# A token assignment that counts on 128 columns and searches in five steps instead of six

## The chip, the cores and the metric

The kernel runs on one core of a Trainium2 chip. The metric is the device time of one execution in microseconds (us); less is better. TensorE (PE) does matrix products, VectorE (DVE), ScalarE (ACT) and GpSimd (POOL) do elementwise work, SyncE (SP) issues the transfers.

## The reference

Three stages follow one another. Only the third one's token assignment is touched by the change.

```python
def _moe2_ref(x, w_gate, w1, w2):
    N, D = x.shape              # 2304 tokens, 512
    E = w_gate.shape[1]         # 8 experts
    cap = N // E                # 288 tokens each
    logits = x @ w_gate
    flat = logits.flatten()
    order = np.argsort(-flat)
    assigned = -np.ones(N, dtype=np.int64)
    counts = np.zeros(E, dtype=np.int64)
    for idx in order:           # the greatest logit first
        tok, e = (int(idx) // E, int(idx) % E)
        if assigned[tok] >= 0 or counts[e] >= cap:
            continue
        assigned[tok] = e
        counts[e] += 1
        if (assigned >= 0).all():
            break
    for e in range(E):
        mask = assigned == e
        h = np.maximum(x[mask] @ w1[e], 0.0)
        out[mask] = h @ w2[e]
```

Ahead of it stand an attention with decay (`x`), and a dense layer `x = leaky(x @ w_in) @ w_out` with 2048 hidden columns.

## The kernel before, in words

The products are made in pairs of rounded parts (`wh`, `gh` high parts, `gl` the remainder), three products for one. The stage that matters here begins when the gate logits `W0` stand (128 partitions x 8 experts x 18 tokens) and ends when the rows of `x2d`, the dense layer's output, and the list `ids` of each expert's tokens are both there; then the first expert gathers its rows.

Two streams share TensorE in this stage. One is `deferred`: 864 products of 512 columns, `acc<-wh,gh` and `acc<-wh,gl`, which make the second half of the dense layer. Each twelve of them need one pair of `gh` (a cast on ACT, L446) and `gl` (a subtraction on POOL, L447). Every other bank of them leaves through `xo` (L1006) to `x2d`.

The other is `routing`. It takes seven phases and a last, shorter one. In each phase every token bids for its best open expert, and a threshold is searched for in the bids' 32-bit keys, in two halves of the key (L1263). A search step compares the 18 keys of each partition with K candidate values on DVE (`r_ge`, L1266), counts with 18 small products on PE (`q_ct`, stationary `r_ge`, moving `r_oh` of 8 columns), tests the counts on DVE (`r_jk`, `r_most`, `r_found`) and sums the found candidates on PE (`q_base`, one product with the stationary `r_unit`). The next compare reads `q_base`. Before, a half has three steps with K of 63, 31 and 31, so a phase has six. After the second half come two counting products (`q_misc`, with `r_on` and `r_tru`) and about twenty small DVE operations that set up the next phase; the last of them is `r_oh`. After the phases, `q_misc` with `r_tri` and 18 products with `r_ob` make the list `ids`.

PE runs in program order. The order is set by numbers: `routing` is a generator that yields, ahead of each of its PE groups, an estimate in ns of the DVE work that precedes the group, and the caller deals products of `deferred` for it (L1057 to L1060):

```python
for ns in routing(nc, rt, ids, ps, W0, mm, vec):
    slack += 1.62 * ns
    while slack > 108 and next(rest, None):
        slack -= 216
```

So in front of a 31-column count stand 8 products of 512 columns, in front of `q_base` 3 or 4, and between two phases 39. What is left over is dealt after `ids`.

Of the kernel before, what the change touches and what calls it, by code (L numbers as in the profile page):

```python
# [14 lines left out]
BF = mybir.dt.bfloat16  # L15
I32 = mybir.dt.int32
AF = mybir.ActivationFunctionType
OP = mybir.AluOpType
# [33 lines left out]
SB = 4  # L52
PBUF = 4
ZG = 60


class InOrder:
# [162 lines left out]
def tile_kernel(ctx, tc, q, k, v, f, w_in, w_out, w_gate, w1, w2, out):  # L220
# [788 lines left out]
    with ExitStack() as c2:  # L1009
        g1p = c2.enter_context(tc.tile_pool(name="g1", bufs=1, reuse_waits="tile"))  # L1010
        g1 = [g1p.tile([128, NF, GT], FT, name=f"g1_{g}") for g in range(NG)]
        psa = c2.enter_context(tc.tile_pool(name="psa", bufs=1, reuse_waits="tile", space=PSUM))
        W0 = cst.tile([128, E, NT], FT, name="W0")
        with tc.tile_pool(name="ps2", bufs=1, reuse_waits="tile", space=PSUM) as psp, \
                tc.tile_pool(name="raw2", bufs=1, reuse_waits="tile") as rawp:
            raw[:] = rawp, W64[2]
            ps = {t: (lambda t=t, n=n: psp.tile([128, 512], FT, name=t, tag=t, bufs=n)) for t, n in (("h", 2), ("T", 2))}
            plan = Plan()
            op = plan.op
            plan.depth = {"T": 2, "h": 2, "x": 2, "w64": W64[2], "wsq": 1, "wbits": 2, "wst": 2, "w": WB, "wt": 1, "wq": 1}  # L1020
            plan.chained = dict.fromkeys(("x", "w64", "wsq", "wbits", "wst", "w", "wt", "wq"))
            for c in range(NC):
                wi[c]["ops"], wi[c]["wb"] = [], []
            wo = [w_out_ops(op, 1, jj, Z2[0] + Z2[1] * jj, "vec", ps) for jj in range(NF // 2)]
            wo0 = [again_ops(op, wod[jj], ZG, "vec") for jj in range(NF // 4)]
            gate = [y for s in wo for y in s["gate"]]
            lasts = []
            for g in range(NG):
                z = 10 * g
                X, loads, xb = x_ops(op, lambda: xp, g, z - 15) if g else (x0[0], [], op("vec", 0, lambda: None, (), -1e6, ["x"]).got)  # L1030
                need = []
                for j in range(NF):
                    need.append(leaky_ops(op, ps, "h", wi, j, lambda X=X: X, (loads, xb), z, z + j, lambda g=g, j=j: g1[g][:, j, :], (), [])[0])
                z = max(z + 8, Z2[2] + Z2[3] * g)
                lasts.append(logits_ops(op, ps, [lambda g=g, i=i: g1[g][:, 2 * i:2 * i + 2] for i in range(NF // 2)], NF, gate + need, [], z, z, g, False))
            lp = psa.tile([128, 512], FT, name="acc", tag="acc", bufs=ACB)

            def tokens(g):
                for i in (2 * g, 2 * g + 1):
                    pe.matmul(lp[:, E * i:E * i + E], L[:, 128 * i:128 * i + 128], sel, start=True, stop=True)  # L1040
            o = [op("pe", 430, lambda g=g: tokens(g), lasts[g:g + 1], 200) for g in range(NG)]
            op("vec", 215, lambda: vec.tensor_copy(W0, lp[:, :NT * E].rearrange("p (i e) -> p e i", e=E)), o, 200)
            run(plan)
        xpool.__exit__(None, None, None)
        lpool.__exit__(None, None, None)
        ps = c2.enter_context(tc.tile_pool(name="ps2b", bufs=1, reuse_waits="tile", space=PSUM))
        gtp = c2.enter_context(tc.tile_pool(name="gt2", bufs=1, reuse_waits="tile"))
        rt = c2.enter_context(tc.tile_pool(name="rt", bufs=1, reuse_waits="tile"))

        def mm(*a, **k):  # L1050
            tc.keep_in_program_order(PE.matmul(*a, **k))  # L1051

        ids = cst.tile([96, NTOK // 96], I32, name="ids")
        wo0 += [{"w": split_weights([(0, 1024, wod[jj])], V)} for jj in range(NF // 4, NF // 2)]
        rest = deferred(ps, mm)
        slack = 0
        for ns in routing(nc, rt, ids, ps, W0, mm, vec):  # L1057
            slack += 1.62 * ns
            while slack > 108 and next(rest, None):
                slack -= 216  # L1060
        for _ in rest:
            pass

# [103 lines left out]
def routing(nc, wk, ids, ps, W0, mm, vec):  # L1167
# [9 lines left out]
    def T(n, *shape, dt=FT, bufs=1):  # L1177
        return wk.tile([128, *shape], dt, name="r_" + n, tag="r_" + n, bufs=bufs)

    def Q(n, w, bufs=1):  # L1180
        return ps.tile([128, w], FT, name="q_" + n, tag="q_" + n, bufs=bufs)
# [9 lines left out]

    io = T("io", 96)
    G.iota(io, pattern=[[1, 96]], base=0, channel_multiplier=0, allow_small_or_imprecise_dtypes=True)
    steps = []
    unit = T("unit", 128, dt=BF)
    found = T("found", 1, dt=BF)
    G.memset(found, 0.0)
    on = T("on", 128, dt=BF)
    G.memset(on, 1.0)
    for i, (stp, K) in enumerate(((1024.0, 63), (32.0, 31), (1.0, 31))):  # L1200
        t = T(f"step{i}", K)
        V.tensor_scalar(t, io[:, 1:K + 1], stp, None, op0=OP.mult)
        G.memset(unit[(0, 64, 96)[i]:], stp)
        steps.append((K, t, (0, 64, 96)[i]))
    we = T("we", E)
    V.tensor_scalar(we, io[:, :E], -1.0, float(E), op0=OP.mult, op1=OP.add)
    eo = T("eo", E)
# [2 lines left out]
    G.affine_select(tri, on, pattern=[[1, 128]], base=0, channel_multiplier=-1, compare_op=OP.is_gt, fill=0.0)  # L1210
    tru = T("tru", 128, dt=BF)
    V.tensor_tensor(tru, on, tri, op=OP.subtract)
    seg = T("seg", E, NT)
    G.memset(seg, 1.0)
    G.memset(seg[:, :, 0:1], 0.0)

    yield 2500
    As = T("A", E, NT, dt=BF)
    G.memset(As, 0.0)
    U = T("U", NT)  # L1220
# [14 lines left out]
    for ph in range(E):  # L1235
# [16 lines left out]
        V.tensor_scalar(k1, b, 31, -0x80000000, op0=OP.arith_shift_right, op1=OP.bitwise_or)  # L1252
        V.tensor_tensor(k1, b, k1, op=OP.bitwise_xor)
        k2 = T("k2", 2, NT, dt=I32)
        V.tensor_scalar(k2[:, 0], k1, 16, None, op0=OP.logical_shift_right)
        V.tensor_scalar(k2[:, 1], k1, 0xffff, None, op0=OP.bitwise_and)
        kf = T("kf", 2, NT)
        V.tensor_copy(kf, k2)
        key = kf[:, 0]
        for half in range(2):  # L1260
            base = None
            for n, (K, kt, at0) in enumerate(steps):
                ct = Q("ct", 512, 2)[:, :E]  # L1263
                ge = T("ge", NT, 63, dt=BF)
                s = [128, NT, K]
                V.scalar_tensor_tensor(ge[:, :, :K], key[:, :, None].to_broadcast(s), base if n else 0.0,  # L1266
                                       kt[:, None, :].to_broadcast(s), op0=OP.subtract, op1=OP.is_ge)
                yield 500 + 19 * K
                for i in range(NT):
                    mm(ct[:K], ge[:, i, :K], oh[:, :, i], start=i == 0, stop=i == NT - 1)  # L1270
                jk, most = T("jk", E), T("most", 1)
                V.tensor_tensor_reduce(out=jk[:K], in0=ct[:K], in1=nr[:K], scale=1.0, scalar=-3e38, op0=OP.add, op1=OP.max, accum_out=most[:K])
                V.tensor_scalar(found[at0:at0 + K], most[:K], 0.0, None, op0=OP.is_ge)
                base = Q("base", 512)[:, 0:1]
                yield 430
                mm(base, unit[:at0 + K], found[:at0 + K], start=True, stop=True)
            yield 480 * (half == 0)
            if half == 0:
                k3 = T("k3", NT)
                V.tensor_scalar(k3, key, base, 131072.0, op0=OP.subtract, op1=OP.mult)  # L1280
                V.tensor_tensor(k3, k3, kf[:, 1], op=OP.add)
                key = k3
        at, eqt = T("at", E, NT, dt=BF), T("eqt", E, NT, dt=BF)
# [2 lines left out]
        with nc.allow_low_precision("counts of at most 18"):  # L1286
            V.tensor_reduce(rs[:, 0], at, axis=AX.X, op=OP.add)
        tot = Q("misc", 512)
        yield 900
        mm(tot[:, :E], on, rs[:, 0], start=True, stop=True)  # L1290
        V.scalar_tensor_tensor(eqt, bi(key), base, oh, op0=OP.is_equal, op1=OP.mult)
        with nc.allow_low_precision("counts of at most 18"):
            V.tensor_reduce(rs[:, 1], eqt, axis=AX.X, op=OP.add)
        yield 400
        mm(tot[:, E:2 * E], tru, rs[:, 1], start=True, stop=True)
        rp = T("rp", E)
        V.tensor_tensor(rp, r, tot[:, :E], op=OP.subtract)
# [15 lines left out]
        G.tensor_scalar(nr, rp, 0.5, -1e6, op0=OP.is_lt, op1=OP.mult)  # L1313
        G.tensor_scalar(r, rp, 0.0, None, op0=OP.max)
        G.tensor_tensor(nr, nr, r, op=OP.subtract)
        yield 3500


    NA, NB = NTOK // 96, 96
# [3 lines left out]
    tot = Q("misc", 512)  # L1323
    yield 500
    mm(tot[:, :E], tri, rs[:, 0], start=True, stop=True)
    yield 3000
    inc = running(As)
    lim = T("lim", E)
    V.tensor_tensor(lim, eo, tot[:, :E], op=OP.add)
# [6 lines left out]
    V.tensor_scalar(na, na, 12582912.0, 12582912.0, op0=OP.add, op1=OP.subtract)  # L1336
    nb = T("nb", NT)
    V.scalar_tensor_tensor(nb, na, -96.0, df, op0=OP.mult, op1=OP.add)
    it = T("it", NT)
    G.iota(it, pattern=[[1, NT]], base=0, channel_multiplier=0, allow_small_or_imprecise_dtypes=True)  # L1340
    ip = T("ip", 1)
    G.iota(ip, pattern=[[0, 1]], base=0, channel_multiplier=1, allow_small_or_imprecise_dtypes=True)
    ga = T("ga", NT, NA, dt=BF)
    V.tensor_tensor(ga, na[:, :, None].to_broadcast([128, NT, NA]), io[:, None, :NA].to_broadcast([128, NT, NA]), op=OP.is_equal)
    oa = T("ge", NT, 2, NA, dt=BF)
    G.tensor_scalar(oa[:, :, 1], ga, ip[:, 0:1], None, op0=OP.mult)
    V.tensor_tensor(oa[:, :, 0], ga, it[:, :, None].to_broadcast([128, NT, NA]), op=OP.mult)
    p = Q("misc", 512)
    for i0 in range(0, NT, 6):
        ob = T("ob", 6, NB, dt=BF, bufs=2)  # L1350
        s = [128, 6, NB]
        V.tensor_tensor(ob, nb[:, i0:i0 + 6, None].to_broadcast(s), io[:, None, :].to_broadcast(s), op=OP.is_equal)
        yield 600
        for i in range(i0, i0 + 6):
            mm(p[:NB, :2 * NA], ob[:, i - i0, :], oa[:, i].rearrange("p a n -> p (a n)"), start=i == 0, stop=i == NT - 1)
    idf = T("idf", NA)
    V.tensor_copy(idf[:NB], p[:NB, NA:2 * NA])
    vec.scalar_tensor_tensor(ids, p[:NB, :NA], 128.0, idf[:NB], op0=OP.mult, op1=OP.add)

# [23 lines left out]
```

## Time and profile before

| | |
|---|---|
| median of 3 runs | 963.43 us (962.97 to 964.17) |
| the profiled execution's own time | 962.55 us |
| its span | 960.8 us |
| the stage: first of the 864 products to the end of the last | 464.5 to 714.2 us |

The span runs from the first to the last instruction; the 1.75 us around it belong to the execution. All sums below are made against the 962.55 us, and the median stands 0.9 us above it.

### The profile page before, as it was taken

To read this page: it belongs to the slowest core of one execution; us is meant where nothing else is said; L and a number is where in the kernel's file an instruction comes from. 1 tells how busy PE (TensorE), PEld (TensorE's weight loads), DVE (VectorE), ACT (ScalarE), POOL (GpSimd) and SP (SyncE) were. 2 spreads that over 40 slices of the span, in tenths; PEclk is the share of its full clock that TensorE was granted. 3 is DMA by queue.
4 is the path that set the end of the run, shared out by engine and by line. 5 is a ranking of instruction groups with operands and counts; after the bars stand their busy time and mean duration, and the time that the engine had idled before them with its cause. 6 is when DMAs were issued, how large, how long until landed. Compare 5 with 4: busy or idle time off the path is not lost.

```text
span 960.8 us, 21226 instructions
## 1 busy us (share of the span) xinstructions
PE 915.5 (95%) x7923; PEld 806.7 (84%) x7923; DVE 571.4 (59%) x1591; ACT 424.9 (44%) x1077; POOL 442.7 (46%) x568
## 2 busy tenths in 40 slices
PE   5999989999999999999999999999978999999996
PEld 4887878878999989999777777777658999999996
DVE  6798877737888378433353654457364656566631
ACT  6998878962333233323222221223224555455521
POOL 6588875567987068000643444445753122212101
PEclk9999999999999999999999999999997999999999
DMA  5666665449975554432312221211335666657511
GB/s 126 168 182 178 176 183 166 137 150 345 302 247 194 158 169 149 126 89 73 115 55 57 66 66 46 66 56 56 110 104 159 193 189 190 194 180 223 168 49 34
DMA packets 140375, 136.78 MB, mean 142 GB/s; under 512 B 69456, under 2 KB 98640, under 8 KB 140272
## 3 DMA queue, kind: packets, MB, share of 16 engines
q1 hardware_dynamic: 137200, 125.99, 43.5%
q0 software_dynamic: 3072, 9.44, 3.5%
q8 instruction: 62, 1.02, 0.4%
q14 instruction: 41, 0.34, 0.1%
HBM read 104.57 MB, written 30.65 MB: 141 GB/s over the span
## 4 chain that ended last, share of the span: by engine, by line
PE 66%; issue 10%; DVE 9%; ACT 6%; DMA 4%; POOL 3%; SPq 1%; POOLq 0%; ACTq 0%; DVEq 0%
PE h L65 20%; PE acc L1051 20%; PE h L1107 7%; PE y L1120 6%; PE s L65 4%; ACT kept L65 4%; PE T L65 3%; PE q_ct L1051 3%; DMA w<-in_moe_w_in 2%; DVE kept L65 2%; DVE wbits L65 2%; ACT P L65 1%; POOL out L1128 1%; DMA X<-xd 1%; SPq L65 1%
## 5 line engine op out<-in xcount | busy, mean ns | idle before, releaser
L65 PE MATMUL h<-X,wh 128*128 128x256 f32 x1728 | 216.5, 284 | 5.2 <-DVE g L65 3.0
L65 PEld LDWEIGHTS h<-X,wh 128*128 128x128 f32 x1728 | 207.5, 189 | 12.7 <-DVE g L65 8.7
L1051 PE MATMUL acc<-wh,gh 128*128 128x512 f32 x576 | 190.3, 404 | 0.0
L447 POOL TENSOR_TENSOR gl<-g,gh 128x512 fp32r<-128x512 f32 x72 | 97.0, 1348 | 111.1 <-ACT gh L446 99.9
L65 ACT ACTIVATE g<-h 128x256 f32<-128x256 f32 x144 | 55.3, 384 | 165.9 <-PE h L65 165.8
L1051 PEld LDWEIGHTS acc<-wh,gh 128*128 128x128 f32 x576 | 109.7, 191 | 20.6
L1107 PE MATMUL h<-XE,wh 128*128 128x288 f32 x768 | 119.5, 305 | 0.3 <-ACT XE L1098 0.3
L1051 PE MATMUL acc<-wh,gl 128*128 128x512 f32 x288 | 119.2, 414 | 0.0
L446 ACT CAST gh<-g 128x512 fp32r<-128x512 f32 x72 | 44.5, 621 | 162.2 <-PE acc L1051 131.6
L347 ACT CAST wh<-wst 128x512 fp32r<-128x512 f32 x132 | 79.8, 620 | 80.1 <-DMA wst<-in_moe_w 44.4
L65 DVE TENSOR_TENSOR wh<-wst,wh 128x512 fp32r<-128x512 f32 x132 | 90.8, 712 | 37.1 <-ACT wh L347 28.3
L1107 PEld LDWEIGHTS h<-XE,wh 128*128 128x128 f32 x768 | 107.5, 193 | 0.6 <-ACT XE L1098 0.6
L65 DVE TENSOR_TENSOR g<-g,h 128x256 f32<-128x256 f32 x144 | 59.9, 417 | 79.1 <-ACT g L65 78.9
L65 ACT ACTIVATE kept<-kept,nm 128x192 f32<-128x192 f32 (+2 forms) x192 | 97.0, 508 | 5.0 <-DVE nm L65 4.3
L1120 PE MATMUL y<-eh,wh 128*128 128x288 f32 x512 | 98.4, 296 | 0.0
L1128 POOL DMA_INDIRECT out<-yo,ids x24 | 24.6, 1026 | 129.5 <-DVE yo L1127 120.0
L1120 PEld LDWEIGHTS y<-eh,wh 128*128 128x128 f32 x512 | 79.6, 188 | 0.2 <-ACT eh L1111 0.2
L65 DVE SCALAR_TENSOR_TENSOR wbits<-w,wbits 128x256 int32<-128x256 int32 x128 | 71.7, 560 | 2.3
L65 POOL TENSOR_TENSOR wst<-wsq,wbits 128x256 f32<-128x256 f32 x64 | 50.3, 785 | 43.1 <-DVE wbits L65 39.3
L65 DVE CUSTOM_DVE_ANT_0 kept<-s,mask 128x192 f32<-128x192 f32 (+4 forms) x160 | 59.5, 422 | 15.7 <-PE s L65 14.8
L1120 PE MATMUL y<-el,wh 128*128 128x288 f32 x256 | 68.0, 296 | 0.0
L1051 PEld LDWEIGHTS acc<-wh,gl 128*128 128x128 f32 x288 | 55.2, 192 | 10.9 <-issue 2.0
(195 smaller groups left out, 1618.6 us busy)
## 6 DMA issues: line engine op xcount, KB each, us to landing
wst<-in_moe_w SPq DMA_DIRECT2D x128, 256.0 KB
X<-xd SPq DMA_DIRECT2D x11, 1024.0 KB
gd<-g SPq DMA_DIRECT2D x36, 256.0 KB
g<-gd SPq DMA_DIRECT2D x36, 256.0 KB
w<-in_moe_w_in SPq DMA_DIRECT2D x32, 256.0 KB
w<-in_moe_w_out SPq DMA_DIRECT2D x32, 256.0 KB
xd<-xt SPq DMA_DIRECT2D x16, 320.0 KB
R<-invd SPq DMA_DIRECT2D x32, 144.0 KB
```

The source lines that it names most:

```text
L65: r = getattr(self.engine, name)(*a, **k)
L347: A.copy(r[u][0], x)
L446: A.copy(gh, g)
L447: G.tensor_tensor(gl, g, gh, op=OP.subtract)
L1051: tc.keep_in_program_order(PE.matmul(*a, **k))
L1107: PE.matmul(h[:, :CAP], w, X[:, c, x, :], start=n == 0, stop=n == 3 * NC - 1)
L1120: PE.matmul(yt[c][:, :CAP], w[:, s], a, start=j == 0 and n == 0, stop=j == NJ - 1 and n == 2)
L1128: sd = G.indirect_dma_start(out=out[:, :], out_offset=bass.IndirectOffsetOnAxis(ap=ids[:, 3 * e + t:3 * e + t + 1], axis=0), in_=y, in_off ...
```

## The change

- The two halves of the key are cut at bit 13 instead of bit 16. The upper half (19 bits) is searched in steps of K = 127, 63, 63, the lower one (13 bits) in two steps of K = 127 and 63: five steps in a phase.
- A count always has 128 stationary columns: the compare writes into one buffer `many` with a stride of K+1, and each product reads 128 columns from there; what lies beyond K is masked when the found candidates are summed.
- `found` holds the step's value, one column for each step of a half. `q_base` is made of one product for each step so far, with the stationaries `rows` (ones in the first K rows); those of the earlier steps stand right behind the count.
- The numbers yielded and the factors change: 1.1 ns for 1, 228 for one product.
- The set-up is shorter on DVE and longer on POOL (the step values come from `iota`). `many` is cleared only in one column of each 128. Three small tiles share others' memory.

```diff
+PACE = 1.1
         for ns in routing(nc, rt, ids, ps, W0, mm, vec):
-            slack += 1.62 * ns
-            while slack > 108 and next(rest, None):
-                slack -= 216
+            slack += PACE * ns
+            while slack > 114 and next(rest, None):
+                slack -= 228
...
-    for i, (stp, K) in enumerate(((1024.0, 63), (32.0, 31), (1.0, 31))):
-        t = T(f"step{i}", K)
-        V.tensor_scalar(t, io[:, 1:K + 1], stp, None, op0=OP.mult)
-        G.memset(unit[(0, 64, 96)[i]:], stp)
-        steps.append((K, t, (0, 64, 96)[i]))
+    rows = {}
+    for K in (127, 63):
+        rows[K] = T(f"rows{K}", 128, dt=BF)
+        G.affine_select(rows[K], on, pattern=[[0, 128]], base=K - 1, channel_multiplier=-1, compare_op=OP.is_ge, fill=0.0)
+    for i, (stp, K) in enumerate(((4096, 127), (64, 127), (1, 63))):
+        t = T(f"step{i}", K, dt=BF)
+        G.iota(t, pattern=[[stp, K]], base=stp, channel_multiplier=0, allow_small_or_imprecise_dtypes=True)
+        steps.append((float(stp), t))
+    halves = [[(127, *steps[0]), (63, *steps[1]), (63, *steps[2])], [(127, *steps[1]), (63, *steps[2])]]
+    many = T("ge", NT * 128, dt=BF)
+    G.memset(many.rearrange("p (i k) -> p i k", k=128)[:, :, 127:], 0.0)
...
-    yield 2500
+    yield 5000
...
-        V.tensor_scalar(k2[:, 0], k1, 16, None, op0=OP.logical_shift_right)
-        V.tensor_scalar(k2[:, 1], k1, 0xffff, None, op0=OP.bitwise_and)
+        V.tensor_scalar(k2[:, 0], k1, 13, None, op0=OP.logical_shift_right)
+        V.tensor_scalar(k2[:, 1], k1, 0x1fff, None, op0=OP.bitwise_and)
...
-                V.scalar_tensor_tensor(ge[:, :, :K], key[:, :, None].to_broadcast(s), base if n else 0.0,
-                                       kt[:, None, :].to_broadcast(s), op0=OP.subtract, op1=OP.is_ge)
+                V.scalar_tensor_tensor(many[:, :NT * (K + 1)].rearrange("p (i k) -> p i k", k=K + 1)[:, :, :K], key[:, :, None].to_broadcast(s), base if n else 0.0,
+                                       kt[:, None, :K].to_broadcast(s), op0=OP.subtract, op1=OP.is_ge)
+                base = Q("base", 512)[:, 0:1]
                 yield 500 + 19 * K
                 for i in range(NT):
-                    mm(ct[:K], ge[:, i, :K], oh[:, :, i], start=i == 0, stop=i == NT - 1)
+                    mm(ct, many[:, (K + 1) * i:(K + 1) * i + 128], oh[:, :, i], start=i == 0, stop=i == NT - 1)
+                for x in range(n):
+                    mm(base, rows[kinds[x][0]], found[:, x:x + 1], start=x == 0, stop=False)
...
-                V.tensor_scalar(found[at0:at0 + K], most[:K], 0.0, None, op0=OP.is_ge)
-                base = Q("base", 512)[:, 0:1]
-                yield 430
-                mm(base, unit[:at0 + K], found[:at0 + K], start=True, stop=True)
+                V.tensor_scalar(found[:, n:n + 1], most, 0.0, stp, op0=OP.is_ge, op1=OP.mult)
+                yield 550
+                mm(base, rows[K], found[:, n:n + 1], start=n == 0, stop=True)
...
-        yield 900
+        yield 1750
         mm(tot[:, :E], on, rs[:, 0], start=True, stop=True)
...
-        yield 400
+        yield 300
         mm(tot[:, E:2 * E], tru, rs[:, 1], start=True, stop=True)
...
-        yield 3500
+        yield 7000
...
-    yield 3000
+    yield 6500
```

How the order moves is shown at three places. In the listing of the changed kernel line numbers are a few higher. The first place is DVE in the second half of a phase; before, a third step like the second one follows:

```order
L1266 SCALAR_TENSOR_TENSOR r_ge<-r_k_7551,r_step_7333 128x1134
L1272 ISA r_jk,r_most<-q_ct,r_nr 63x8
L1272 ISA r_most 63x1
L1273 TENSOR_SCALAR r_found<-r_most 63x1
L1266 SCALAR_TENSOR_TENSOR r_ge<-r_k_7551,q_base,r_step_7336 128x18x31
L1272 ISA r_jk,r_most<-q_ct,r_nr 31x8
```

And of the change, where the half ends with these rows and the next phase's set-up follows:

```order
L1270 SCALAR_TENSOR_TENSOR r_ge<-r_k_7556,r_step_7337 128x18x127
L1279 ISA r_jk,r_most<-q_ct,r_nr 128x8
L1279 ISA r_most 128x1
L1280 TENSOR_SCALAR r_found<-r_most 128x1
L1270 SCALAR_TENSOR_TENSOR r_ge<-r_k_7556,q_base,r_step_7339 128x18x63
```

Each compare has become twice as long (2286 and 1134 elements in place of 1134 and 558), and there is one fewer in this half. In the first half three compares stay three.

The second place is PE behind a count. Before, it is alike in every step (here a half's second one): the count's last product, three or four products of the other stream, and the sum:

```order
L1051 MATMUL q_ct<-r_oh,r_ge 31x8
L1051 MATMUL acc<-wh,gh 128x512
L1051 MATMUL acc<-wh,gl 128x512
L1051 MATMUL acc<-wh,gh 128x512
L1051 LDWEIGHTS r_unit
L1051 MATMUL q_base<-r_found,r_unit 128x1
```

Of the change, behind the count of a half's third step:

```order
L1052 MATMUL q_ct<-r_oh,r_ge 128x8
L1052 LDWEIGHTS r_rows_7331
L1052 MATMUL q_base<-r_found,r_rows_7331 128x1
L1052 LDWEIGHTS r_rows_7333
L1052 MATMUL q_base<-r_found,r_rows_7333 128x1
L1052 MATMUL acc<-wh,gh 128x512 x2
L1052 MATMUL acc<-wh,gl 128x512
L1052 LDWEIGHTS r_rows_7333
L1052 MATMUL q_base<-r_found,r_rows_7333 128x1
```

Two sums of earlier steps have come in right behind the count (one in a second step, none in a first). Two or three products of the other stream stand in front of the last sum (of 35 places, 18 have two), 8 or 9 in front of a 63-column compare's count, 16 or 17 in front of the lower half's first count, 48 instead of 39 between two phases, and 8 or 9 instead of 7 in front of `r_on`.

The third place is PE at the stage's end. Before, the 18 products with `r_ob` (a list of 96 columns) follow the last of the 864:

```order
L1051 MATMUL q_misc<-r_rs,r_tri 128x8
L1051 MATMUL acc<-wh,gl 128x512
L1051 MATMUL acc<-wh,gh 128x512 x2
...
L1051 LDWEIGHTS r_ob
L1051 MATMUL q_misc<-r_ge,r_ob 96x48
```

Of the change, where the tile is part of `many` and is called `r_ge`:

```order
L1052 MATMUL q_misc<-r_ge 96x48
L1052 MATMUL acc<-wh,gh 128x512
L1052 MATMUL acc<-wh,gl 128x512
L1052 MATMUL acc<-wh,gh 128x512
L1052 LDWEIGHTS r_ge
```

Those 18 products now come in three groups of six among the 864, with three products between the groups; 36 instead of 30 products stand in front of `r_tri`, 34 instead of 22 behind it, and the last 14 follow the third group.

## Rows read from the trace of the kernel before

**Rows 1.** The page: busy us by engine, share of the span, instructions.
```profile
PE 915.5 (95%) x7923; PEld 806.7 (84%) x7923; DVE 571.4 (59%) x1591; ACT 424.9 (44%) x1077; POOL 442.7 (46%) x568
```

**Rows 2.** Busy us by engine in stretches (phases), granted clock, DMA share, GB/s.
```profile
573.20:606.30 33.10, 33.10 (x236) 24.71 (x236) 16.93 (x51) 7.88 (x14) 15.19 (x14) 1.00 0.21 65
639.40:675.00 35.60, 33.20 (x233) 24.78 (x234) 22.11 (x51) 9.59 (x16) 19.84 (x19) 1.00 0.20 59
675.00:700.70 25.70, 25.68 (x195) 18.65 (x195) 8.95 (x30) 7.77 (x13) 17.23 (x14) 0.93 0.46 127
```

**Rows 3.** The chain in order of time, 500 to 545 us: start, us, what.
```profile
506.54 0.69 PE q_ct L1051 x18
507.23 0.90 PE acc L1051 x3
508.12 0.11 PE q_base L1051
508.23 2.04 PE acc L1051 x8
510.27 0.57 PE q_ct L1051 x18
510.84 0.89 PE acc L1051 x3
511.73 0.02 PE q_base L1051
511.75 1.96 PE acc L1051 x8
...
531.21 8.95 PE acc L1051 x39
```

**Rows 4.** Weight loads by shape, 464 to 716 us: busy us, mean ns, idle before.
```profile
L1051 PEld LDWEIGHTS <-r_ge 128*31 128x31 bf16 x504 | 15.0, 95 | 10.3 <-issue 9.0 <-DVE r_ge L1266 1.2
L1051 PEld LDWEIGHTS <-r_ge 128*63 128x63 bf16 x252 | 9.4, 114 | 7.0 <-issue 5.8 <-DVE r_ge L1266 1.3
L1051 PEld LDWEIGHTS <-r_ob 128*96 128x96 bf16 x18 | 1.0, 124 | 0.9 <-DVE r_ob L1352 0.7 <-issue 0.2
L1051 PEld LDWEIGHTS <-r_on 128*128 128x128 bf16 x7 | 0.7, 95 | 1.9 <-issue 1.9
```

**Rows 5.** Instructions of the tile r_ge: ns min/median/max, first and last start.
```profile
L1266 DVE SCALAR_TENSOR_TENSOR r_ge<-r_k,q_base,r_step x14: 804/805/1911, 487.8 to 694.7; 128x558 bf16<-128x558 f32 x14
L1266 DVE SCALAR_TENSOR_TENSOR r_ge<-r_kf,r_step x7: 1327/1340/1342, 468.7 to 672.4; 128x1134 bf16<-128x1134 f32 x7
```

**Rows 6.** The timeline of DVE, 511 to 516.5 us: two compares.
```profile
511.80 0.81 DVE L1266 SCALAR_TENSOR_TENSOR r_ge<-r_kf,q_base,r_step 128x558 bf16<-128x558 f32 x1 [0.58 <-PE q_base L1051]
515.96 1.34 DVE L1266 SCALAR_TENSOR_TENSOR r_ge<-r_k,r_step 128x1134 bf16<-128x1134 f32 x1
```

**Rows 7.** What PE waited for, 464 to 716 us: us, times, longest.
```profile
PE q_ct L1051 <- DVE r_oh L1245: 2.1, 1, 2.1
PE q_misc L1051 <- DVE r_rs L1322: 1.2, 1, 1.2
```

**Rows 8.** The timelines of POOL and DVE, 636 to 678 us: a compare behind a subtraction.
```profile
653.31 1.28 POOL L447 TENSOR_TENSOR gl<-g,gh 128x512 fp32r<-128x512 f32 x1 [1.94 <-PE acc L1051]
...
653.77 1.41 DVE L1266 SCALAR_TENSOR_TENSOR r_ge<-r_k,q_base,r_step 128x558 bf16<-128x558 f32 x1 [0.65 <-PE q_base L1051]
```

**Rows 9.** The chain in order of time, behind the seventh phase's wait and at the end.
```profile
676.76 3.55 PE acc L1051 x8
...
708.97 5.13 PE acc L1051 x22
714.17 0.59 ACT xo L1006
714.78 2.60 DMA x2d<-xo
```

**Rows 10.** The timeline of DVE at the end: the list of tokens is written.
```profile
715.97 0.18 DVE L65 SCALAR_TENSOR_TENSOR ids<-q_misc,r_idf 96x24 int32<-96x24 f32 x1
```

More of the change, by code (lines that the diff above doesn't have):

```diff
@@ L1193, in routing @@
     G.iota(io, pattern=[[1, 96]], base=0, channel_multiplier=0, allow_small_or_imprecise_dtypes=True)
[L1194 to L1197, printed above, removed]
+    found = T("found", 3, dt=BF)
     on = T("on", 128, dt=BF)
     G.memset(on, 1.0)
-    for i, (stp, K) in enumerate(((1024.0, 63), (32.0, 31), (1.0, 31))):
-        t = T(f"step{i}", K)
-        V.tensor_scalar(t, io[:, 1:K + 1], stp, None, op0=OP.mult)
-        G.memset(unit[(0, 64, 96)[i]:], stp)
-        steps.append((K, t, (0, 64, 96)[i]))
+    rows = {}
+    for K in (127, 63):
+        rows[K] = T(f"rows{K}", 128, dt=BF)
+        G.affine_select(rows[K], on, pattern=[[0, 128]], base=K - 1, channel_multiplier=-1, compare_op=OP.is_ge, fill=0.0)
+    steps = []
+    for i, (stp, K) in enumerate(((4096, 127), (64, 127), (1, 63))):
[5 more added lines that the diff above has]
+    G.memset(many.rearrange("p (i k) -> p i k", k=128)[:, :, 127:], 0.0)
     we = T("we", E)
@@ L1212, in routing @@
     V.tensor_tensor(tru, on, tri, op=OP.subtract)
-    seg = T("seg", E, NT)
+    seg = T("seg", E, NT, dt=BF)
     G.memset(seg, 1.0)
     G.memset(seg[:, :, 0:1], 0.0)
-    yield 2500
+    yield 5000
     As = T("A", E, NT, dt=BF)
@@ L1260, in routing @@
         for half in range(2):
-            base = None
-            for n, (K, kt, at0) in enumerate(steps):
+            base, kinds = None, halves[half]
+            for n, (K, stp, kt) in enumerate(kinds):
                 ct = Q("ct", 512, 2)[:, :E]
-                ge = T("ge", NT, 63, dt=BF)
                 s = [128, NT, K]
-                V.scalar_tensor_tensor(ge[:, :, :K], key[:, :, None].to_broadcast(s), base if n else 0.0,
-                                       kt[:, None, :].to_broadcast(s), op0=OP.subtract, op1=OP.is_ge)
+                V.scalar_tensor_tensor(many[:, :NT * (K + 1)].rearrange("p (i k) -> p i k", k=K + 1)[:, :, :K], key[:, :, None].to_broadcast(s), base if n else 0.0,
+                                       kt[:, None, :K].to_broadcast(s), op0=OP.subtract, op1=OP.is_ge)
+                base = Q("base", 512)[:, 0:1]
                 yield 500 + 19 * K
                 for i in range(NT):
-                    mm(ct[:K], ge[:, i, :K], oh[:, :, i], start=i == 0, stop=i == NT - 1)
+                    mm(ct, many[:, (K + 1) * i:(K + 1) * i + 128], oh[:, :, i], start=i == 0, stop=i == NT - 1)
+                for x in range(n):
+                    mm(base, rows[kinds[x][0]], found[:, x:x + 1], start=x == 0, stop=False)
                 jk, most = T("jk", E), T("most", 1)
-                V.tensor_tensor_reduce(out=jk[:K], in0=ct[:K], in1=nr[:K], scale=1.0, scalar=-3e38, op0=OP.add, op1=OP.max, accum_out=most[:K])
-                V.tensor_scalar(found[at0:at0 + K], most[:K], 0.0, None, op0=OP.is_ge)
-                base = Q("base", 512)[:, 0:1]
-                yield 430
-                mm(base, unit[:at0 + K], found[:at0 + K], start=True, stop=True)
+                V.tensor_tensor_reduce(out=jk, in0=ct, in1=nr, scale=1.0, scalar=-3e38, op0=OP.add, op1=OP.max, accum_out=most)
+                V.tensor_scalar(found[:, n:n + 1], most, 0.0, stp, op0=OP.is_ge, op1=OP.mult)
+                yield 550
+                mm(base, rows[K], found[:, n:n + 1], start=n == 0, stop=True)
             yield 480 * (half == 0)
@@ L1279, in routing @@
                 k3 = T("k3", NT)
-                V.tensor_scalar(k3, key, base, 131072.0, op0=OP.subtract, op1=OP.mult)
+                V.tensor_scalar(k3, key, base, 16384.0, op0=OP.subtract, op1=OP.mult)
                 V.tensor_tensor(k3, k3, kf[:, 1], op=OP.add)
@@ L1338, in routing @@
     V.scalar_tensor_tensor(nb, na, -96.0, df, op0=OP.mult, op1=OP.add)
-    it = T("it", NT)
+    it = T("mw", NT)
     G.iota(it, pattern=[[1, NT]], base=0, channel_multiplier=0, allow_small_or_imprecise_dtypes=True)
@@ L1344, in routing @@
     V.tensor_tensor(ga, na[:, :, None].to_broadcast([128, NT, NA]), io[:, None, :NA].to_broadcast([128, NT, NA]), op=OP.is_equal)
-    oa = T("ge", NT, 2, NA, dt=BF)
+    many = T("ge", NT * 128, dt=BF)
+    oa = many[:, :2 * NT * NA].rearrange("p (i a n) -> p i a n", a=2, n=NA)
     G.tensor_scalar(oa[:, :, 1], ga, ip[:, 0:1], None, op0=OP.mult)
@@ L1349, in routing @@
     for i0 in range(0, NT, 6):
-        ob = T("ob", 6, NB, dt=BF, bufs=2)
+        at0 = 2 * NT * NA + i0 % 12 * NB
+        ob = many[:, at0:at0 + 6 * NB].rearrange("p (i n) -> p i n", n=NB)
         s = [128, 6, NB]
-        V.tensor_tensor(ob, nb[:, i0:i0 + 6, None].to_broadcast(s), io[:, None, :].to_broadcast(s), op=OP.is_equal)
+        V.tensor_tensor(ob, nb[:, i0:i0 + 6, None].to_broadcast(s), io[:, None, :NB].to_broadcast(s), op=OP.is_equal)
         yield 600
@@ L1355, in routing @@
             mm(p[:NB, :2 * NA], ob[:, i - i0, :], oa[:, i].rearrange("p a n -> p (a n)"), start=i == 0, stop=i == NT - 1)
-    idf = T("idf", NA)
+    idf = T("kf", NA)
     V.tensor_copy(idf[:NB], p[:NB, NA:2 * NA])
```

## The prediction

> **What bounds the kernel now.** I read the page first: PE is busy in 95% of the span [rows 1], so a stage can only get shorter where PE has work less or waits less. Then I cut the stage that the change touches into its phases. In an undisturbed phase PE is busy 33.10 of 33.10 us, DVE 16.93, ACT 7.88 and POOL 15.19 [rows 2]: PE sets the pace, and DVE, which carries the search, has slack in the sum. Last I read the chain in order of time for one phase [rows 3]. It runs through PE alone: product after product of the other stream (`acc`), with the counts (`q_ct`) and sums (`q_base`) put in between. So what the routing costs is not DVE's time but the room that its small products take on PE, and the few places where PE really waits for DVE.
>
> The room first. 39 products in 8.95 us are 0.2295 us each, the switch behind them included. A step with K = 63 is 0.69 + 0.90 + 0.11 + 2.04 = 3.74 us for 11 products, which by themselves are 2.52: it adds 1.22 us. A step with K = 31 is 0.57 + 0.89 + 0.02 + 1.96 = 3.44, and adds 0.92 [rows 3]. A phase has two of the first and four of the second: 2 x 1.22 + 4 x 0.92 = 6.12 us. Check: 117 products are 26.85, with 6.12 that is 32.97, and the phase took 33.1 [rows 2].
>
> The waits second. PE waited 2.1 us once for `r_oh`, ahead of the seventh phase, and 1.2 us for `r_rs` in front of `r_tri` [rows 7]. In the stretch with the first wait POOL is busy 19.84 us instead of 15.19, since the first expert's weights are split there, and the phase is 35.60 us instead of 33.10 [rows 2]. Behind the wait eight products took 3.55 us [rows 9] instead of 2.04 [rows 3]: 1.5 us lost, in the stretch whose mean granted clock is 0.93 [rows 2], so part of it ran at the lower level, 1.2 GHz.
>
> The end third. The last product ends at 714.17, its copy takes 0.59 and its store 2.60, so the rows of `x2d` stand at 717.4 [rows 9], while the list `ids` is written by 716.2 [rows 10]. The gather needs both and follows the store. An earlier end of the 864 products is therefore an earlier gather, as long as the list keeps ahead.
>
> **The change, part by part.** The 864 products stay; only what stands between them changes.
>
> *Five steps for six, and 128 columns.* The open price is that of a count of 18 products with 128 stationary columns each. Loads with 31, 63 and 96 columns take 95, 114 and 124 ns, growing with the columns, but the load of 128 (`r_on`) takes 95, like that of 31 [rows 4]. A full load of this type is thus seen to go faster than one of 96. These are single loads, never 18 in a row, so I bound the count: from below by the 0.57 us of the 31-column one; from above by the line through 0.57 / 18 = 31.7 ns at 31 columns and 0.69 / 18 = 38.3 ns at 63 [rows 3], 0.21 ns a column, which gives 52 ns at 128 and 0.93 us for 18. I take 0.57, because the 128-column load's row lies on the 31-column one. I take the small step's other costs too (0.92 in all): the larger `q_base` cost, 0.11, stands in the K = 63 steps alone, whose sum reads 63 rows; the new sums read all 128.
>
> The Trainium skill ("TensorE: Matmul & The Clock Gate", section on the weight-path perf modes) says that a load goes by the fast path when it has 128 columns and its type isn't FP32; by that rule the count is as I take it, and the 95 ns beside the 124 agree. The same page's section on LDWEIGHTS has the time grow with the column count alone; by that the count would be the dearest possible, and this row speaks against it.
>
> The early sums are four in a phase, small products in a group that has begun. 31.7 ns bounds one from above (it has one column to move instead of eight): 0.12 us in a phase. A phase now adds 5 x 0.92 + 0.12 = 4.72 us instead of 6.12: 1.40 less, in seven phases **-9.8 us** (with the upper price of the count, 35 x 0.36 = 12.6 less of that, and a loss of 2.8).
>
> *Longer compares.* From 558 to 1134 elements a compare goes from 805 to 1340 ns [rows 5], 0.93 ns an element; 2286 elements are 2.41 us by this slope, 2.70 in proportion. K = 63 with a base in PSUM I take as 1.34 to 1.40. The cover is the products dealt in front of the count. Short compare: it starts 0.05 us behind the sum (511.80 against 511.75) [rows 3, 6], and eight products give 1.96 us: 0.5 us to spare. Lower half's first compare: it starts 0.5 us behind its sum (515.96; the eight products from 511.75, a count and the four products and sum behind it end near 515.4) [rows 3, 6], and 16 products give 3.7: 0.5 to 0.8 to spare. First compare of a phase: 48 products instead of 39, 2.07 us more cover for 1.1 to 1.4 us more compare. All three cost nothing while POOL stays away. When the compare meets a subtraction on POOL it does not: a compare begun at 653.77, with POOL busy until 654.59, took 1.41 instead of 0.81 [rows 8], the worst 1.91 [rows 5]. Six of 28 short compares were over 1.4 us. Before, 8 products behind 0.81 us hid nearly all of that; now 0.5 us is hidden, and a delay of 0.6 to 1.1 leaves 0.1 to 0.6. A fifth of 28 compares at 0.35 is 2.0 us, most of it in the seventh phase, where POOL is busiest: **+2.0 us** (0 to 6). What waits behind PE's count is the other stream itself, so these waits go straight into the stage.
>
> *Between the phases and at the end.* Six of the seven set-ups of DVE were covered by 39 products and are by 48. In the last, PE's 2.1 us become 2.1 + 1.2 - 2.1 = 1.2: **-0.9**; I leave the 1.5 us of slow clock where they are. In front of `r_tri` 36 products stand instead of 30, 1.4 us more cover than the 1.2 us wait needs: **-1.2**. Two products in front of a last sum instead of three take 0.23 us of cover away, but the tested counts were ready in time: I take 0, and 18 x 0.1 = 1.8 as the upper end. The 18 products of the list now stand ahead of the last 14 `acc`: six of them at about 45 ns (the line above at 96 columns) and two switches at 0.18 (half of 0.92 - 0.57), 0.45 for each of three groups: **+1.3**. The list is then ready while 14 products (3.2 us) still run, and stays ahead of the store.
>
> *The set-up.* DVE loses three small multiplications, POOL gets three more pattern writes and two selections of the size of its others. 38 products stand in front of the first count, 8.7 us; the first compare, 2.4 to 2.7 us, began at 468.7 [rows 5] and would end by 471.4, while PE is at that count some 10 us behind 464.5. Nothing.
>
> Sum: -9.8 + 2.0 - 0.9 - 1.2 + 1.3 = -8.6 us. Against the profiled execution, 962.55 - 8.6 = 953.95; the median of the runs stands 0.9 above it: **954.8 us**.
>
> **The rivals.**
> - *The columns are paid for after all* (slower). If 18 loads in a row take 52 ns each, the five counts cost 0.93 us each and 12.6 us come back: 967.4. It decides from 0.57 + 8.6 / 35 = 0.82 us a count on. For it: the loads of 31, 63 and 96 grow in order. Against it: the 95 ns at 128 [rows 4], seen on single loads only.
> - *DVE becomes the bound.* The 21 short compares have 0.5 us to spare where they had 1.1. If they come 0.3 us late on average, by longer strides or because POOL's rhythm of one subtraction in twelve products falls on them, PE waits 6.3 us instead of 2.0: 959.1. For it: DVE is now dealt little more than it takes. Against it: DVE's busy time is half of a phase [rows 2].
> - *POOL's collisions fall elsewhere.* All positions move; if the compares miss the subtractions and the seventh phase's wait with its slow clock goes too, 2.0 + 1.2 + 1.5 = 4.7 more are won: 950.1.
> - *The gain doesn't reach the end*: another load sets the gather. The store was last by 1.2 us before and will be by more, so I give this no chance of its own.
>
> **How the numbers follow.** My forecast, 951.5 to 958, has a chance of 0.66, the second rival (958 to 961) 0.15, the third (949 to 951.5) 0.10, the first 0.09. A change of 0.2%, 1.9 us, is about what a measurement of this kernel can tell from none. Faster by more: forecast, third, and nearly all of the second, 0.88; within it: 0.04, between the second and the first; slower: 0.08. The range from 950 to 961 leaves out the first rival and some of the third.
>
> **What would show it.** The chain of an undisturbed phase: 112 products in 30.4 us instead of 117 in 33.1; the count's piece 0.57 us (0.93 if the first rival holds); its loads near 95 ns. PE's waits for the compare: some 2 us in total, and near 6 in the second rival. The wait of `r_tri` gone; 1 us left for `r_oh`. The last `acc` near 705.5, and the gather as far behind it as before. The prediction is wrong if the counts show more than 0.8 us, or if the waits for DVE in the steps outgrow the 9.8 us that the steps give.

## The result, and the profile after

The changed kernel takes 951.62 us (median of 4 runs, 951.3 to 953.11), the kernel before 963.8 us beside it (4 runs, 962.97 to 969.1). The ratio is 0.9865, with a 95% interval of 0.9828 to 0.9902: faster by 1.35%. That is 3.2 us below the predicted time and 0.1 us inside the lower end of the predicted range. The profiled span went from 960.8 to 950.1 us. PE lost 12.3 us of busy time against [rows 1]; DVE and POOL gained 28.6 and 19.4. POOL's gain is not new work: its 72 subtractions `gl` take 118.7 us instead of 97.0 by the pages, 1653 ns each instead of 1348. The page now:

```profile
PE 903.2 (95%) x7818; PEld 802.8 (84%) x7818; DVE 600.0 (63%) x1560; ACT 425.7 (45%) x1077; POOL 462.1 (49%) x570
```

The stage of the 864 products ran from 464.48 to 714.17 us before, 249.7 us, and runs from 466.81 to 703.22 now, 236.4 us: 13.3 us less. It begins 2.3 us later, although nothing is ordered otherwise ahead of it; in the other runs of this document it begins anywhere between 465.33 and 471.24 us, so I take this for spread. What lies behind it takes 246.9 instead of 246.6 us. So the stage holds the whole gain.

The chain in order of time through an undisturbed phase (start, us, what), to be laid beside [rows 3]:

```profile
566.07 0.48 PE q_ct L1052 x18
566.55 0.79 PE acc L1052 x3
567.34 0.02 PE q_base L1052
567.36 1.96 PE acc L1052 x8
...
584.62 11.01 PE acc L1052 x48
595.63 0.48 PE q_ct L1052 x18
```

A count takes 0.48 us, with four times as many columns as the 0.57 us one before. The three products behind it take 0.79 instead of 0.89 or 0.90 us. One step is 0.48 + 0.79 + 0.02 + 1.96 = 3.25 us; less its eleven products (2.52) it adds 0.73 us, where I had taken 0.92. From count to count the phase is 595.63 - 566.07 = 29.56 us for 112 products; at 0.2295 us these are 25.70, so the routing adds 3.86 us. Taken in the same way, the undisturbed phase before is 606.29 - 573.23 = 33.06 us for 117 products (26.85), 6.21 us of routing; the prediction's 6.12 are its steps alone. The two counts:

```profile
573.23 0.69 PE q_ct L1051 x18
606.29 0.69 PE q_ct L1051 x18
```

Weight loads by shape, from 464 to 716 us (busy us, mean ns, idle before), beside [rows 4]:

```profile
L1052 PEld LDWEIGHTS <-r_ge 128*128 128x128 bf16 x630 | 18.8, 96 | 12.6 <-DVE r_ge L1270 7.9 <-issue 4.7
```

The 95 ns that were seen on single loads [rows 4] hold for 18 in a row, at 96.

What PE waited for in the stage (us, times, longest), in place of [rows 7]:

```profile
PE q_ct L1052 <- DVE r_ge L1270: 2.7, 3, 2.1
PE q_misc L1052 <- POOL r_ge L1353: 1.9, 1, 1.9
```

The waits for `r_oh` and in front of `r_tri` are gone, and so are two short ones for `r_rs` (L1287 before), 0.6 us in all, which [rows 7] does not show. Before, the set-up that ends with `r_oh` was over at 674.97 us, and four of the first expert's subtractions on POOL (L348) began between 662.70 and 672.36, in the midst of it; now it is over at 653.37, and they begin at 653.16 (L349). Two other waits have come. The long one of the first row is in the seventh phase. The timelines of DVE and POOL there (start, us, engine, line, operation):

```profile
663.39 0.82 DVE L1286 TENSOR_SCALAR r_k<-r_kf,q_base 128x18 f32<-128x18 f32 x1 [0.50 <-PE q_base L1052]
664.24 1.22 DVE L1287 TENSOR_TENSOR r_k<-r_k,r_kf 128x18 f32<-128x18 f32 x1
665.49 3.58 DVE L1270 SCALAR_TENSOR_TENSOR r_ge<-r_k,r_step 128x2286 bf16<-128x2286 f32 x1
...
665.38 1.29 POOL L349 TENSOR_TENSOR wh<-wst,wh 128x512 fp32r<-128x512 f32 x1
666.64 3.57 POOL L448 TENSOR_TENSOR gl<-g,gh 128x512 fp32r<-128x512 f32 x1
```

The compare, 2.54 us elsewhere, is issued 0.11 us after a subtraction has begun on POOL and takes 3.58 us, about 1.0 more. The next subtraction is issued just before the first one ends and takes 3.57 instead of 1.29 us: it ends 1.14 us behind the compare. They go one after the other, not side by side. The Trainium skill ("SBUF — State Buffer", section on SBUF's two separate sides) calls the port pair that these engines share an exclusive lock, which an instruction holds from its start to its end; the rows of the compare and of these two subtractions agree.

The compare is the smaller part of the delay. Its two small operations on `r_k` (L1286 and L1287), which lie between the sum and the compare, take 0.24 and 0.18 us in the median of the seven phases and 0.82 and 1.22 here, beside subtractions on POOL: 1.6 us more. With the compare's 1.0 that is 2.6 us. Less the 0.5 to 0.8 us that the prediction had to spare, this accounts for the wait of 2.06.

The chain at that place and at the stage's end:

```profile
665.49 3.59 DVE r_ge L1270
669.09 0.05 issue
669.13 0.64 PE q_ct L1052 x18
669.78 1.48 PE acc L1052 x3
671.25 0.03 PE q_base L1052
671.28 2.68 PE acc L1052 x8
...
693.43 2.41 POOL r_ge L1353
695.84 0.04 issue
695.88 0.41 PE q_misc L1052 x6
696.29 1.07 PE acc L1052 x3
697.36 0.44 PE q_misc L1052 x6
697.80 1.45 PE acc L1052 x3
699.25 0.44 PE q_misc L1052 x6
699.69 3.53 PE acc L1052 x14
```

Behind each of the two waits PE is slow for a while: three products take 1.48 and 1.45 us instead of 0.79, and eight 2.68 instead of 1.96. The granted clock is the column behind POOL's in this view of stretches (busy us by engine, clock, DMA share, GB/s):

```profile
566.30:596.00 29.70, 29.70 (x224) 22.96 (x220) 19.27 (x47) 7.57 (x13) 16.56 (x14) 1.00 0.23 63
655.50:678.00 22.50, 20.44 (x166) 14.93 (x163) 14.59 (x26) 6.53 (x12) 19.62 (x13) 0.92 0.33 94
...
695.90:703.30 7.40, 7.31 (x38) 5.56 (x37) 1.72 (x3) 1.77 (x4) 1.18 (x1) 0.77 0.19 73
```

It is 1.00 in the undisturbed phase, 0.92 around the first wait and 0.77 behind the second, so part of both stretches ran at 1.2 GHz instead of 2.4; PE had been idle for 2.06 and 1.89 us before. At the end the list is late because DVE's set-up of it runs between POOL's subtractions, which follow one another there without a gap from 684.94 to 692.8: an operation such as the second `r_na`, 0.18 us before, takes 1.21.

### The profile page after: what moved, and what is told of

It is laid out like the page before. It is cut to its first block, busy times and chain, and to the rows that moved or that the text cites. A ratio compares the mean times of both kernels' runs of the same rounds, so it can differ in the third digit from the quotient of the medians.

```text
span 950.1 us, 20982 instructions
## 1 busy us (share of the span) xinstructions
PE 903.2 (95%) x7818; PEld 802.8 (84%) x7818; DVE 600.0 (63%) x1560; ACT 425.7 (45%) x1077; POOL 462.1 (49%) x570
## 4 chain that ended last, share of the span: by engine, by line
PE 65%; issue 11%; DVE 9%; ACT 6%; POOL 5%; DMA 5%; SPq 0%; POOLq 0%; ACTq 0%; DVEq 0%
PE acc L1052 21%; PE h L66 20%; PE h L1108 7%; PE y L1121 6%; PE s L66 4%; ACT kept L66 3%; PE T L66 3%; DVE kept L66 3%; DMA w<-in_moe_w_in 2%; DVE wbits L66 2%; PE q_ct L1052 2%; POOL out L1129 1%; ACT P L66 1%; DVE r_ge L1270 1%; DMA X<-xd 1%
## 5 line engine op out<-in xcount | busy, mean ns | idle before, releaser
L448 POOL TENSOR_TENSOR gl<-g,gh 128x512 fp32r<-128x512 f32 x72 | 118.7, 1653 | 76.6 <-ACT gh L447 72.8
L1052 PE MATMUL acc<-wh,gl 128*128 128x512 f32 x288 | 116.5, 404 | 0.0
L348 ACT CAST wh<-wst 128x512 fp32r<-128x512 f32 x132 | 79.8, 620 | 76.6 <-DMA wst<-in_moe_w 42.1
```

The lines of the kernel that those rows point to most:

```text
L348: A.copy(r[u][0], x)
L448: G.tensor_tensor(gl, g, gh, op=OP.subtract)
```

## The experiments

The expectations speak of theory A, that of the prediction: the gain is room on PE, since a load of 128 columns costs no more than a small one. The rivals are that the steps or the dealing make the gain, and, for what was given back, that it was lost to POOL's subtractions or to too little cover. Beside every version the kernel before ran on the same chip; its median was 963.8 to 966.6 us, so ratios are compared, not times.

**127 columns instead of 128** in the changed kernel's counts:

```diff
-                    mm(ct, many[:, (K + 1) * i:(K + 1) * i + 128], oh[:, :, i], ...)
+                    mm(ct[:127], many[:, (K + 1) * i:(K + 1) * i + 127], oh[:, :, i], ...)
```

> The changed kernel, its counts with 127 stationary columns instead of 128 (found row 127 left out, the candidates are all in the first 127 rows); five steps and the dealing stay. Theory A (a count is cheap because its weights have the full 128 columns): the piece of a count in the chain goes from 0.48 us to 0.9 or more, plus 0.1 us each for the switch in and out, 35 times 0.45 to 0.6 us: 16 to 21 us back, 967 to 972 us. Rival B (the gain is that of five steps for six and of the dealing, the column count plays no part): 951 to 953 us.

Measured: 967.15 us, ratio 1.0035 (1.0014 to 1.0055); the gain is gone. The loads by shape (busy us, mean ns, idle before):

```profile
L1052 PEld LDWEIGHTS <-r_ge 128*127 128x127 bf16 x630 | 42.8, 141 | 6.6 <-DVE r_ge L1271 2.7
```

A count in the chain:

```profile
510.44 1.03 PE q_ct L1052 x18
```

One column less makes a load 141 ns instead of 96 and a count 1.03 us instead of 0.48. 35 counts are 19.3 us dearer; against the changed kernel 16.4 us show by the two ratios (1.0035 and 0.9865), and the stage is 252.9 us instead of 236.4. The slower counts also give DVE time: PE waits 0.7 us for compares instead of 2.7. The Trainium skill ("TensorE: Matmul & The Clock Gate", section on the weight-path perf modes) ties the fast load to just 128 columns of a type that isn't FP32: this pair of rows agrees.

**The kernel before with 128-column counts**, six steps and the old dealing kept (what lies beyond K is cut off when the counts are tested):

```diff
+    wide = T("ge", NT * 64 + 64, dt=BF)
+    G.memset(wide, 0.0)
-                ge = T("ge", NT, 63, dt=BF)
+                ge = wide[:, :NT * (K + 1)].rearrange("p (i k) -> p i k", k=K + 1)
-                    mm(ct[:K], ge[:, i, :K], oh[:, :, i], ...)
+                    mm(ct, wide[:, (K + 1) * i:(K + 1) * i + 128], oh[:, :, i], ...)
```

> The kernel before with its six steps, K and dealing, but with 128 stationary columns in each count (the rows beyond K are not used). Theory A: a K = 31 step gets from 3.44 us to about 3.25 for its 11 products, a K = 63 step from 3.74 to about 3.45, 28 x 0.19 + 14 x 0.3 = 9.5 us, 954 us. Rival B: no change, 963 us.

Measured: 955.96 us, ratio 0.9905 (0.9885 to 0.9926). A large step in its chain:

```profile
512.28 0.48 PE q_ct L1051 x18
512.76 0.79 PE acc L1051 x3
513.55 0.11 PE q_base L1051
513.66 2.04 PE acc L1051 x8
```

By the rows, 14 large steps save 0.21 at the count and 0.11 behind it and 28 small ones 0.09 and 0.10, 9.8 us in all; 0.95% of the time is 9.2.

**The kernel before with the first sum of a half over 128 rows** instead of 63:

```diff
+    one = T("one", 128, dt=BF)
+    G.memset(one, 0.0)
+    G.memset(one[:64], 1024.0)
-                mm(base, unit[:at0 + K], found[:at0 + K], start=True, stop=True)
+                mm(base, unit[:at0 + K] if n else one, found[:at0 + K] if n else found, start=True, stop=True)
```

> The kernel before, only the first step's sum reads all 128 rows (zeros beyond 63) instead of 63. If the 0.11 us of q_base and the 2.04 instead of 1.96 us behind it, which stand in the K = 63 steps alone, come from the sum's 63 rows: 14 x 0.17 = 2.4 us, 961 us. If they come from the 63-column count ahead of it: no change, 963 us.

Measured: 961.61 us, ratio 0.9968 (0.9951 to 0.9986). The chain behind a half's first count:

```profile
508.00 0.90 PE acc L1051 x3
508.89 0.02 PE q_base L1051
508.92 1.96 PE acc L1051 x8
```

The sum takes 0.02 instead of 0.11 us, the eight products behind it 1.96 instead of 2.04 [rows 3]: 14 times 0.17 is 2.4 us, 0.32% is 3.1.

**Both in the kernel before** (and the mask `seg` in bf16 as in the change, for room in memory); still six steps, dealt as before.

> The kernel before with both: 128 stationary columns in each count and 128 rows in each sum, still six steps in a phase and the old dealing (a mask tile is kept in the smaller type to make room). If the two parts add up, 9 and 3 us come off: 951.5 to 952.5 us, and five steps for six together with the new dealing are worth nothing beside it. If five steps and the dealing bring their own 5 us (seven steps of 0.73 us less on PE): 956 us, since the two parts then overlap.

Measured: 951.31 us, ratio 0.986 (0.9836 to 0.9884), the same as the whole change. Its chain, through an undisturbed phase, has the steps of the changed kernel:

```profile
570.48 0.48 PE q_ct L1051 x18
570.96 0.79 PE acc L1051 x3
571.75 0.02 PE q_base L1051
571.77 1.96 PE acc L1051 x8
...
601.80 0.48 PE q_ct L1051 x18
```

PE's waits are those of [rows 7]:

```profile
PE q_ct L1051 <- DVE r_oh L1250: 2.1, 1, 2.1
PE q_misc L1051 <- DVE r_rs L1327: 1.2, 1, 1.2
```

So the load and the rows of the sum alone give as much as the whole change. What five steps add can be read from the rows. From count to count a phase of this run, 117 products, takes 601.80 - 570.48 = 31.32 us. Less the products (26.85) that is 4.47 us of routing; the changed kernel has 3.86, so five steps should give 4.3 us in seven phases. The waits that went give 3.9 (2.1, 1.2 and the short ones of 0.6), and the slow products behind the first of them 1.6 (1.25 + 3.06 us for eleven here, instead of 0.79 + 1.96). Against these 9.8 us stand the 8.75 that the changed kernel loses in the seventh phase (2.7 and 1.4) and at the list (4.65, below). Its stage is 236.4 us long and this one's 237.6 (467.15 to 704.73); in the time no difference shows.

**The changed kernel with the old dealing**: the factors 1.62, 108, 216 and the old numbers yielded.

```diff
-PACE = 1.1
+PACE = 1.62
-            while slack > 114 and next(rest, None):
-                slack -= 228
+            while slack > 108 and next(rest, None):
+                slack -= 216
-    yield 5000
+    yield 2500
...
```

> The changed kernel with the dealing numbers of before (1.62, 108, 216, and the old yields). The products then run out at the start of the seventh phase. If the dealing is part of the gain: the seventh phase and the list run bare on DVE, five steps of about 2.9 us, a set-up of 8 and a list of 10, some 33 us behind the last product instead of none, the list ready about 15 us later than now, 966 us, with PE waiting for every compare there. If the steps' room on PE alone counts: 952 us.

Measured: 961.15 us, ratio 0.9976 (0.9958 to 0.9993). The longer compares draw 13 products instead of 8 by these numbers, and the 864 run out in front of the seventh phase's first count. PE's two largest waits in the stage, in total:

```profile
PE q_ct L1052 <- DVE r_ge L1270: 7.6, 4, 3.1
PE q_misc L1052 <- POOL r_ge L1353: 5.0, 1, 5.0
```

The loss was less than expected, but the new dealing is needed with five steps: it is worth 1.1% there.

**The first expert's low parts made on DVE instead of POOL**, in the changed kernel:

```diff
-            lo_on = G if e == 0 else vec
+            lo_on = V if e == 0 else vec
```

> The changed kernel, the first expert's weights split on DVE instead of POOL. If PE's late waits (2.1 us for a compare in the seventh phase, 1.9 us in front of the list's products) come from those splits holding DVE up: both go, with the slow clock behind them, 946 to 948 us. Rival: the splits stand in DVE's order in front of the search or behind it and make the chain or the first expert late, 953 us or more.

Measured: 946.12 us, ratio 0.9798 (0.9773 to 0.9823). The stage is 231.6 us. PE's waits:

```profile
PE q_ct L1052 <- DVE r_ge L1270: 1.2, 3, 0.5
PE q_base L1052 <- DVE r_found L1280: 1.1, 1, 1.1
```

The row of the lower half's first compare (ns min/median/max):

```profile
L1270 DVE SCALAR_TENSOR_TENSOR r_ge<-r_k,r_step x7: 2543/2543/2545, 486.0 to 665.4; 128x2286 bf16<-128x2286 f32 x7
```

The chain with the list's products:

```profile
693.22 0.78 PE acc L1052 x3
694.01 0.25 PE q_misc L1052 x6
...
695.29 3.28 PE acc L1052 x14
```

The stretched compare (3.58 us) is back at 2.54, the wait for `r_ge` at the end is gone, and the list's products run at full clock: what was given back, was given back to these subtractions. DVE does POOL's 14 subtractions of this stage for it. The price is the second of the two waits: two of these subtractions stand on DVE in front of the test of a count (667.84 to 670.21 us), and PE waits 1.1 us for `r_found`.

**More products dealt late**: 6000 instead of 7000 yielded between the first phases, 2000 more in front of the seventh phase's stretched compare, 10500 instead of 6500 in front of the list.

> The changed kernel with other numbers of products: 43 instead of 48 between the first seven phases' ends and beginnings, 26 instead of 16 in front of the seventh phase's compare of the lower half, 53 instead of 34 behind r_tri. If the waits are a matter of cover alone: 2.1 + 1.9 us of waits and some 3 us of slow clock behind them go, 944.5 to 947 us. Rival: the longer set-ups no longer fit into 43 products (they left 1.6 us at the tightest) and waits appear there, 951 us.

Measured: 949.47 us, ratio 0.9827 (0.9802 to 0.9851), above what was expected. The long wait is gone (six short ones for compares, 2.4 us in total, none over 0.5), but PE now waits 0.7 us for `gl` and 0.7 for `r_rs`. Cover moved is cover missing elsewhere.

**Only the last number changed**, so that no product is left behind the list:

```diff
-    yield 6500
+    yield 9400
```

> The changed kernel, only the last 14 products moved ahead of the list's products (48 instead of 34 behind r_tri). The wait of 1.9 us and the slow clock behind it (1.4 us) go: 948.5 us. Rival: the list becomes the last to be ready in place of the store, and the gain is lost: 951 us.

Measured: 948.74 us, ratio 0.9827 (0.9801 to 0.9852), as expected. The store of `x2d` begins at 701.26 instead of 703.90. Not all of that is the list. The wait for the stretched compare, 2.1 us, is here as before, ahead of anything that this edit moves, but the three products behind it take 0.79 us and the granted clock from 656 to 680 us is 1.00: 1.4 us that the changed kernel's profile lost there are not lost in this one. So a wait of this length is not followed by the lower clock in every run.

**Both of these together**: low parts on DVE, and 9400.

> The changed kernel with the first expert's low parts made on DVE, and all remaining products dealt ahead of the list. If the two losses of the changed kernel are separate ones (the compare of the seventh phase behind POOL's subtractions, and the set-up of the list that runs without cover), the single gains add up in part: about 943 to 945 us, 0.976 to 0.979 of the time before. If they are the same loss, the list's set-up being late only through POOL, the time is that of the version with the subtractions on DVE alone, 946 us, or above it, since products in front of the list now delay the list.

Measured: 946.1 us, ratio 0.9789 (0.976 to 0.9818), no better than the first alone. The two losses were one: the list was late through POOL, and with POOL out of the way the cover adds nothing.

**Six steps with the low parts on DVE**: the kernel before with both 128-wide edits and this one.

> The kernel before with 128-column counts and full-row sums, six steps and the old dealing, and the first expert's low parts made on DVE. If five steps for six do save room on PE that the changed kernel loses to POOL's subtractions, this version now stays behind the changed kernel with the same edit (946.1 us) by 3 to 5 us: 949 to 951. If a step fewer is worth nothing in itself, or the longer compares take as much as it saves, the two are within 1.5 us: 945 to 947.5.

Measured: 947.58 us, ratio 0.9819 (0.9789 to 0.9848), between the two expectations. The long wait for `r_oh` is gone, and of that in front of `r_tri` little is left:

```profile
PE q_misc L1051 <- DVE r_rs L1327: 0.3, 1, 0.3
```

So both waits of [rows 7] came from POOL's subtractions too. By the medians this version is 1.5 us behind the five-step kernel of the run above, and the intervals overlap. The stages, one profile each, are 232.9 us here (465.39 to 698.29) and 231.6 in the five-step kernel with the low parts on DVE. By the rows the 4.3 us of room should leave 1.9 there: PE waits 2.3 us in that kernel's stage and 0.9 in this one's, and 18 list products, 0.95 us, stand among its 864; it is 1.3 shorter. The medians don't settle what five steps are worth once POOL is out of the way: neither nothing nor the 4.3 us is excluded.

## Why the prediction was right, point by point

- **The mechanism** was right: the routing costs its room on PE, and a load of 128 columns goes like one of 31. The 127-column run takes the gain back with one column less.
- **The steps, -9.8 us**, were sized too low. The step that failed is "I take 0.57, because the 128-column load's row lies on the 31-column one", with 0.57 as the bound from below, and the 0.92 us for a step that followed. The count takes 0.48, below the bound, and the products behind it 0.10 less. From count to count a phase's routing is 3.86 us instead of 6.21: 2.35 less, where I had 1.40, and 16.5 us in seven phases.
- **Which part of it gains**: I put five steps and 128 columns into one term. The six-step runs part them: columns and full-row sums alone reach the whole net gain. The step fewer frees 4.3 us on PE by the rows, which the waits behind POOL's subtractions take back; in the time it could not be measured.
- **Compares meeting POOL, +2.0 us**: PE waits 2.7 us in three places, 2.06 of it in the seventh phase as said. That the size fits is luck. I counted short compares (28 of them, the number before; the changed kernel has 21), and these make 0.6 us in two places. The 2.06 stand in front of the lower half's first compare, which I had at nothing, and more of it comes from the two small operations ahead of the compare than from the compare. Not foreseen were also the lower clock behind it (1.48 + 2.68 instead of 0.79 + 1.96, 1.4 us) and that it takes the place of the 1.5 us that were lost like this before and that I left where they were.
- **`r_oh`, -0.9, and `r_tri`, -1.2**: both waits went whole, 2.1 and 1.2 us, and the two short ones for `r_rs`, 0.6, which I had not counted. I put this down to more products in front of them; the last run shows that with POOL's subtractions away the two long ones go at 39 and 30 products too, but for 0.3 us.
- **The list's products, +1.3 us**: 0.41 + 0.44 + 0.44 = 1.29 for themselves; the 20 products between and behind them took 6.05 instead of 4.59, 1.46 more, and in front of them stood a wait of 1.9 that I had at nothing. 4.65 in all.
- **The sum**: -16.5 + 2.7 + 1.4 - 1.5 - 2.1 - 1.2 - 0.6 + 4.65 = -13.15 us; the stage is 13.3 shorter. The prediction came near because errors on either side met: the steps gave 6.7 us more than I had and the waits that went 1.8 more, and the compares and the list took 4.05 more. That the time fell inside the range is luck in part.
- **The rivals**: paying for the columns did not happen (0.48 against the 0.82 that decides). DVE as the bound did not either: the 21 short compares were not 0.3 us late on average, PE waited three times in all. The end followed, as said: the gather starts at 707.43, behind the store.

## What to carry to other kernels

Before a small product's stationary matrix is made narrower to save work, try the full 128 columns and rows, with zeros or unread results beyond: in such a chain of small bf16 products the wide form was the cheaper one, and it alone gave what it gave together with a new search and a new dealing. Where DVE works just in time, look at what POOL has in the same stretch, since 14 subtractions moved off it were worth more here than one step less. And take a switch between two streams as a price of its own, read from the products behind it.

## What the runs showed of the hardware that was not expected

A count of 18 loads and 8-column products takes 0.48 us with 128 columns, 0.57 with 31, 0.69 with 63 and 1.03 with 127: the cost grows with the columns and falls by more than half at the last one. The switch to the other stream does not follow that cost: three of its products take 0.90 us behind a count with 31 or 63 columns, 0.80 with 127 (at 511.47 us in that run) and 0.79 with 128. A sum over 63 rows costs 0.17 us more than one over 128, its wake included, 14 times in the kernel before. Little of the counts' difference shows in the rows of their products: one takes 176 ns on average with 128 columns, 176 with 31 and 178 with 63; only with 127 it is 202. The small operations that stand between POOL's subtractions belong here too: 1.2 us for one that takes 0.18 elsewhere.
